# First scan of an SSD kernel: two masks change engines, the scores and the gains are reordered, one weight piece is finished in two steps

## The chip, the cores and the metric

One core of one Trainium2 chip. The metric is the device time of one execution in microseconds (us). Beside the three timed runs there is one profiled execution; its trace gives the start and duration of every instruction.

## The reference, cut to what matters

A Mamba-2 SSD scan over 4 batches of 8 heads, 768 steps, head width 32, state width 16, in chunks of 32; its output, as 3072 rows of 256, goes through a two-layer network with a quick GELU.

```python
cum = np.cumsum(log(clip(a, 1e-6, 1)), axis=-1)         # within a chunk
L = np.exp(cum[..., :, None] - cum[..., None, :]) * causal
y = (C @ B^T * L) @ x + (C @ state) * np.exp(cum)       # inside the chunk, and from the state
state = decay_full * state + sum_j(B_j x_j * decay_from_j)
h = y_rows @ w_in                                       # 256 -> 2048
out = (h * (1 / (1 + np.exp(-1.702 * h)))) @ w_out      # 2048 -> 256
```

The weights arrive as 64-bit floats and are rounded to 32 bits on the chip.

## The kernel before

**Tiles and stages.** The rows are cut into 6 groups of 512 rows; a group is four chunks of 128 rows, and two chunks are a pair. Group 0 is pairs 0 and 1 of batch 0. Its scan has a path of its own, since nothing can hide it: the first 18 us of the span. Then comes `hidden(0, f)` for the 16 blocks f of w_in (two products and one Silu each), then `project_all(0)`, into which the scan of group 1 is put, then groups 1 to 5 with a form that needs fewer products, each with the scan of the next group put in between.

**Order.** Every engine runs its instructions in the order in which the program writes them (`in_order` at the end fixes it). An instruction that waits holds everything behind it on its engine. SP, and at two places ScalarE and GpSimd, issue the DMAs, also in order.

**First scan.** `differ_of` and `decay_exp` (L557) make the decays L of a pair. `turn_first` (L597) transposes B and C on VectorE. `mask_first(p)` (L632) spreads C over the two heads of a row group, on GpSimd. `turn_back` (L609) transposes B back on TensorE, `ends_first` (L478) weighs it with the decay to the end of a half chunk. `score` (L664) makes C B^T of both pairs in one four-bank area `cb`; `since_first` (L515, L520), called between pair 0 and pair 1, makes `since`, the decay from the start. `weigh` (L675) multiplies L by the scores, one VectorE instruction a pair. `gain` (L695) makes A, the increments of the state, of both pairs; `parts_first` (L712) copies them to `steps`, `keep_first` (L717, L725, L726) scans them to the states S. `since_start` (L649) makes CsT on GpSimd. `finish` makes y: `intra` (L818) from L and x, `inter` (L804) from CsT and S; between the two pairs' `intra` stands `fan_all` (L418), which spreads the next pair's decays from the operand X that `pick_a` (L364) made of `az1`. ScalarE copies y to yT (L838). `dense` (L1150) and `pads` (L442) are products of ones whose results nobody reads.

**PSUM banks.** `bank(...)` hands out four banks in turn. In the order of the program the last ones before y are b, rows0, rows1, A0, A1, dense; the four banks of y follow.

**Weights.** They come in pieces: of w_in 0 to 3 with two blocks and 4, 5 with four, of w_out 6 to 9 with four. A piece takes these steps: `fetch` (SP, L181), `fields` (VectorE, L193 and L196: exponent, mantissa), `clamp` (ScalarE, L204 and L205), `rounded` (VectorE, L209), `join` (VectorE, L223 and L229, writes w_in or w_out). `narrow(i)` writes `rounded(i)`, `join(i)` and `fields(i + 1)`: for pieces 2, 4, 5, 6 the join first, for 3 and 7 to 9 `fields(i + 1)` first. Piece 3 is blocks 6 and 7, piece 4 blocks 8 to 11. `fetch(1, held=nc.gpsimd)` begins with a small GpSimd memset of the target (L172), which stands behind `since_start(0)` on GpSimd; SP waits for it, and nine more loads are behind that one on SP's queue.

A table of places, in `in_hidden[0]`, says after which block of `hidden(0, f)` a step is written:

```python
for i, k, c in ((2, 1, 1), (3, 2, 2), (4, 4, 7), (5, 8, 10), (6, 10, 14), (7, 14, 15)):
    at(in_hidden[0], k, lambda i=i: narrow(i))
    at(in_hidden[0], c, lambda i=i: clamp(i + 1))
```

`fold_ident(1)` (L336) fills the second half of a constant of VectorE that the scan of pair 3 reads first, in the projection.

Of the kernel before, what the change touches and what calls it, by code (L numbers as in the profile page):

```python
# [35 lines left out]
def kernel(  # L36
# [99 lines left out]
                out=t[32 * r:32 * r + 32],  # L136
                in_=src[0, Q * r:Q * r + Q, :TG].rearrange("q (i f) n -> i q (f n)", i=32))

    def load(p, parts=None):
        if parts is None:  # L140
            parts = "bcx" if p < 2 * PG else "bx"
            if p >= 2 * PG:
                load_blocks(p)
        for part in parts:
            dst, src, e = {"b": (rb, B, N), "c": (rc, C, N), "x": (rx, x, D)}[part]
            dst[p] = raw.tile([P, 2, NH, e], FP32, tag=part, name=f"{part}{p}",
                              bufs=2 if part == "c" else 3)
            for k in range(2):
                b, c = divmod(2 * p + k, NC)
                sl = slice(c * P, (c + 1) * P)  # L150
                nc.sync.dma_start(out=dst[p][:, k], in_=src[b, :, sl, :].rearrange("h s d -> s h d"))


    assert NF == 4 * CG
# [58 lines left out]

    NEXT = {1: (6,), 5: (9,)}

    def join(i, parts=1):

        name, f, n = PIECES[i]
        n //= parts
        low, m, p2 = bits.pop(i)[1], mantissa.pop(i), power.pop(i)  # L220
        for k in range(parts):
            cols, fs = slice(k * n * DM, (k + 1) * n * DM), slice(f + k * n, f + (k + 1) * n)
            nc.vector.scalar_tensor_tensor(out=p2[:, cols], in0=low[:, cols], scalar=0x80000000,  # L223
                                           in1=p2[:, cols], op0=ALU.bitwise_and, op1=ALU.bitwise_or)
# [4 lines left out]
            nc.vector.scalar_tensor_tensor(  # L229
                out=dst, in0=m[:, cols].bitcast(FP32).rearrange("p (h e) -> p h e", h=h),  # L230
                scalar=2.0 ** -20, in1=p2[:, cols].bitcast(FP32).rearrange("p (h e) -> p h e", h=h),
                op0=ALU.mult, op1=ALU.mult)
        for n in NEXT.get(i, ()):
            fetch(n)

    def narrow(i):
        rounded(i)
        if i in (2, 4, 5, 6):
            join(i, 2 if i in (4, 5) else 1)
        if i == 6:  # L240
            decay_rows(0)
        if i + 1 < len(PIECES):
            fields(i + 1)
        if i not in (2, 4, 5, 6):
            join(i, 2 if i == 3 else 1)


    scratch = dram.tile([NC, 2, NB * NH, H], FP32, name="scratch")
# [41 lines left out]
    load_first("B", [nc.sync] * R)  # L290
    fetch(0)
    load(0, "x")
    load(1, "x")


    edge = const.tile([P, 2], FP32, name="edge")
# [37 lines left out]
    def fold_ident(k, engine=nc.vector):  # L334
# [17 lines left out]
    def clip(t):  # L352

        nc.vector.tensor_scalar(out=t, in0=t, scalar1=1e-6, scalar2=1.0,
                                op0=ALU.max, op1=ALU.min)
        nc.vector.memset(t.rearrange(by_chunk, s=2)[:, :, :, 0], 0.0)
# [65 lines left out]

    def fan_all(p):

        ab = area(f"ab{p}")[:, :, :2 * Q * H]
        for r in range(R):
            fan(p, r, ab[:, r])
        fans[p] = ab

    def decay_fanned(p):  # L430

# [77 lines left out]
    def since_first():  # L509

        since[0] = ssd.tile([P, NC, P], FP32, tag="since", name="since0")
        rows = [bank(f"rows{p}")[:, :2 * P] for p in range(PG)]
        for p in range(PG):
            at = slice(32 * p, 32 * p + 32)
            nc.tensor.matmul(out=rows[p],  # L515
                             lhsT=whose[at, p].rearrange("p h n -> p (h n)"),
                             rhs=cum[at].rearrange("p k s -> p (k s)"), start=True, stop=True,
                             tile_position=(32 * p, 0), skip_group_check=True)
        for p in range(PG):
            nc.scalar.activation(since[0][:, 2 * p:2 * p + 2].rearrange("p c s -> p (c s)"),  # L520
                                 rows[p], AF.Exp)

    def drops():

# [101 lines left out]
    def mask_first(p):  # L626

        s = st[p]
        s["CT"] = ssd.tile([P, 2, Q, P], FP32, tag="CT", name=f"CT{p}")
        if p:  # L630
            nc.vector.memset(s["CT"][:, 0, 0, :1], 0.0)
        nc.gpsimd.tensor_tensor(  # L632
            out=s["CT"], in0=s["tp"].unsqueeze(2).to_broadcast([P, 2, Q, P]),
            in1=part.unsqueeze(1).unsqueeze(3).to_broadcast([P, 2, Q, P]), op=ALU.mult)
# [16 lines left out]
    def score(pairs, between=lambda: None, to=None):  # L651

        cb = (to or area(f"cb{pairs[0]}")).rearrange("p r (k e) -> p r k e", k=2 * PG)
        for n, p in enumerate(pairs):
            s = st[p]
            BT, CT = s["BT"], s.pop("CT")
            s["cb"] = cb[:, :, 2 * n:2 * n + 2]
            if n:
                between()
            for k in range(2):  # L660
                for i, side in enumerate(SIDES):
                    for r in range(R):
                        rows = slice(32 * r, 32 * r + 32)
                        nc.tensor.matmul(  # L664
                            out=s["cb"][side, r, k].rearrange("p (q i) -> p q i", q=Q),
                            lhsT=BT[rows, k, side], rhs=CT[rows, k, :, side],
                            start=True, stop=True, tile_position=(32 * r, H * i),
                            skip_group_check=True)
# [11 lines left out]

        return (4 * p + m + 1) % (2 * NC) == 0

    def gain(pairs, to=None):
# [3 lines left out]
        for n, p in enumerate(pairs):  # L687
            Be = BE.pop(p)[0]
# [12 lines left out]
            increment[p] = [t[:, 2 * n:2 * n + 2] for t in A] if pairs[0] else A  # L701
# [68 lines left out]
    def finish(pairs, steps=range(2)):  # L770
# [38 lines left out]

        def intra(n, p):  # L810
            L = Ls[p]
            for k in range(2):
# [15 lines left out]
        if early:  # L828
            for n, p in enumerate(pairs):
                if n:  # L830
                    fan_all(PG)
                intra(n, p)
            for n, p in enumerate(pairs):
                for i in range(2):
                    inter(n, p, (i,))
            for t in range(NK):
                for i in range(2):
                    nc.scalar.activation(  # L838
                        yT[g][:, t, cols].rearrange("p (k s i) -> p s k i", s=2, i=H)[:, i], y[i][t],
                        AF.Copy)  # L840
# [362 lines left out]
    fields(2)  # L1203
    clamp(2)
    load(PG, "bc")
# [234 lines left out]
```

## Time and profile before

| what | value |
|---|---|
| median of 3 runs | 346.78 us (346.44, 346.78, 349.93) |
| profiled execution | 347.67 us, of it the span 345.9 us |
| granted TensorE clock | 1.00 |
| TensorE busy | 339.2 us, 98% |
| VectorE busy | 256.1 us, 74% (97% from 47 to 80 us) |
| ScalarE busy | 155.1 us, 45% |
| GpSimd busy | 16.7 us, 5% |
| first scan | 0 to 17.89 us |
| hidden layer of group 0 | 17.89 to 46.96 us |

Engines in the trace: PE is TensorE, PEld its weight loads, DVE is VectorE, ACT ScalarE, POOL GpSimd, SP the queue that issues most DMAs; ACTq or SPq is the queue of an engine, where DMAs are issued. A line of the timeline has the start in us, the duration, the engine, the line of the program, the operation with what it writes and reads, and in brackets the time that the engine had waited just before and what ended the wait. An fp32 product is two records of TensorE. A line of the list of waits has who waited for whom, the sum in us, how often, and the longest. A line of the chain of waits has the start, the duration and the step.

### The profile page before, as it was taken

To read this page: it belongs to the slowest core of one execution; us is meant where nothing else is said; L and a number is where in the kernel's file an instruction comes from. 1 tells how busy PE (TensorE), PEld (TensorE's weight loads), DVE (VectorE), ACT (ScalarE), POOL (GpSimd) and SP (SyncE) were. 2 spreads that over 40 slices of the span, in tenths; PEclk is the share of its full clock that TensorE was granted. 3 is DMA by queue.
4 is the path that set the end of the run, shared out by engine and by line. 5 is a ranking of instruction groups with operands and counts; after the bars stand their busy time and mean duration, and the time that the engine had idled before them with its cause. 6 is when DMAs were issued, how large, how long until landed. Compare 5 with 4: busy or idle time off the path is not lost.

```text
span 345.9 us, 8116 instructions
## 1 busy us (share of the span) xinstructions
PE 339.2 (98%) x3380; PEld 270.2 (78%) x3380; DVE 256.1 (74%) x484; ACT 155.1 (45%) x352; POOL 16.7 (5%) x40
## 2 busy tenths in 40 slices
PE   8999999999999999999999999999999999999996
PEld 6633744555788888888888888888888888899996
DVE  5988999999799998858995667787564654465463
ACT  5786771507454324754332554442454322554320
POOL 7300110300000100000000000000000000000000
PEclk9999999999999999999999999999999999999999
DMA  6698899545637100435603036400000300000401
GB/s 160 132 289 211 217 239 133 152 67 102 122 63 127 36 0 15 65 99 100 110 27 51 2 78 121 64 0 3 0 4 2 62 2 0 0 2 0 63 0 62
DMA packets 90004, 25.76 MB, mean 74 GB/s; under 512 B 73416, under 2 KB 87248, under 8 KB 89968
## 3 DMA queue, kind: packets, MB, share of 16 engines
q1 hardware_dynamic: 89104, 24.72, 35.0%
q10 hardware_dynamic: 832, 0.52, 0.5%
q8 instruction: 26, 0.43, 0.5%
q14 instruction: 10, 0.08, 0.1%
q0 software_dynamic: 32, 0.01, 0.0%
HBM read 22.00 MB, written 3.24 MB: 73 GB/s over the span
## 4 chain that ended last, share of the span: by engine, by line
PE 92%; DMA 3%; SPq 2%; DVE 1%; issue 0%; ACT 0%; POOL 0%; DVEq 0%
PE acc L1039 28%; PE X L934 19%; PE Y L944 14%; PE o L976 8%; PE acc L1046 7%; PE h L878 7%; DMA bits<-in_moe_w_in_dram 3%; PE y L818 2%; PE cb L664 2%; SPq L181 1%; PE y L804 1%; PE A L695 1%; PE ab L536 1%; DMA az<-in_a_dram 1%; POOL CsT L649 0%
## 5 line engine op out<-in xcount | busy, mean ns | idle before, releaser
L939 ACT ACTIVATE ac<-X 128x256 f32<-128x256 f32 x76 | 29.1, 383 | 81.7 <-PE X L934 81.0
L1039 PE MATMUL acc<-mg,mw 128*128 128x256 f32 x192 | 54.5, 379 | 0.0
L1066 DVE TENSOR_TENSOR gT<-Y,ac 128x512 f32<-128x512 f32 x38 | 26.2, 689 | 38.1 <-PE Y L944 32.5
L911 ACT ACTIVATE gT<-gT 128x512 f32<-128x512 f32 (+1 forms) x76 | 38.9, 519 | 29.3 <-DVE gT L1066 28.8
L934 PE MATMUL X<-my,mi 128*128 128x256 f32 x152 | 45.2, 380 | 0.0
L1039 PEld LDWEIGHTS acc<-mg,mw 128*128 128x128 f32 x192 | 36.6, 190 | 4.9
L1066 DVE TENSOR_TENSOR gT<-Y,b 128x256 f32<-128x256 f32 x38 | 15.8, 419 | 28.5 <-PE Y L944 28.5
L878 PE MATMUL h<-yT,w_in 128*128 128x512 f32 (+1 forms) x92 | 35.5, 541 | 1.4 <-DVE w_in L229 0.9
L1039 PE MATMUL acc<-gT,w_out 128*128 128x256 f32 x128 | 35.5, 380 | 0.0
L878 PEld LDWEIGHTS h<-yT,w_in 128*128 128x128 f32 x92 | 17.2, 190 | 18.2 <-issue 12.8
L934 PEld LDWEIGHTS X<-my,mi 128*128 128x128 f32 x152 | 28.0, 190 | 4.0 <-ACT ac L939 0.3
L976 PE MATMUL o<-gT,w_out 128*128 128x512 f32 x64 | 28.3, 596 | 0.0
L902 DVE TENSOR_TENSOR mg<-gT 128x512 f32<-128x512 f32 x40 | 27.2, 681 | 0.0
L1039 PEld LDWEIGHTS acc<-gT,w_out 128*128 128x128 f32 x128 | 24.3, 190 | 3.4 <-ACT yT L853 0.2
L939 ACT ACTIVATE b<-X 128x256 f32<-128x256 f32 x38 | 14.6, 383 | 20.8 <-PE X L934 20.3
L934 PE MATMUL X<-yT,w_in 128*128 128x256 f32 x76 | 23.2, 389 | 0.0
L944 PE MATMUL Y<-yT,w_in 128*128 128x256 f32 x76 | 22.7, 381 | 0.0
L944 PE MATMUL Y<-my,mi 128*128 128x256 f32 x76 | 22.7, 381 | 0.0
L934 PE MATMUL X<-my,w_in 128*128 128x256 f32 x76 | 22.5, 380 | 0.0
L944 PE MATMUL Y<-yT,mi 128*128 128x256 f32 x76 | 22.5, 380 | 0.0
L976 PEld LDWEIGHTS o<-gT,w_out 128*128 128x128 f32 x64 | 11.9, 190 | 13.6 <-issue 12.7
L408 DVE TENSOR_TENSOR_SCAN L<-a,idents 128x1024 f32<-128x1024 f32 x9 | 20.5, 2279 | 0.3 <-DMA a<-scratch 0.3
(152 smaller groups left out, 547.8 us busy)
## 6 DMA issues: line engine op xcount, KB each, us to landing
a<-scratch SPq DMA_DIRECT2D x18, 256.0 KB, 4.9
bits<-in_moe_w_out_dram SPq DMA_DIRECT2D x8, 512.0 KB, 7.4
x<-in_x_dram SPq DMA_DIRECT2D x24, 128.0 KB, 3.7
out_dram<-ob SPq DMA_DIRECT2D x40, 64.0 KB, 2.0
bits<-in_moe_w_in_dram SPq DMA_DIRECT2D x8, 256.0 KB, 3.7
bits<-in_moe_w_in_dram SPq DMA_DIRECT2D x4, 512.0 KB, 11.4
b<-in_B_dram SPq DMA_DIRECT2D x20, 64.0 KB, 3.3
af<-in_a_dram SPq DMA_DIRECT2D x3, 384.0 KB
```

The lines of the kernel that those rows point to most:

```text
L408: nc.vector.tensor_tensor_scan(out=L, data0=ra[p].rearrange("p k e -> p (k e)"), data1=idents.rearrange("p h i -> p (h i)"), initial=0.0, ...
L664: nc.tensor.matmul(out=s["cb"][side, r, k].rearrange("p (q i) -> p q i", q=Q), lhsT=BT[rows, k, side], rhs=CT[rows, k, :, side], start=Tru ...
L878: nc.tensor.matmul(out=h[:, cols], lhsT=w_in[:, f, k], rhs=yT[g][:, k, cols], start=(k == 0 and c == 0), stop=(k == NK - 1), skip_group_ch ...
L902: nc.vector.tensor_tensor(out=t[:, 0:2], in0=B[:, :, 1], in1=B[:, 0], op=ALU.subtract)
L911: nc.scalar.activation(o, i, AF.Silu, scale=GELU_SCALE)
L934: nc.tensor.matmul(out=s["X"], lhsT=lhsT, rhs=rhs, start=i == "1", stop=i == "4", skip_group_check=True)
L939: nc.scalar.activation(copy, s["X"], AF.Copy)
L944: nc.tensor.matmul(out=o, lhsT=lhsT, rhs=rhs, start=s.pop("new", False), stop=i != "5", skip_group_check=True)
L976: nc.tensor.matmul(out=o[c], lhsT=w_out[:, c, f], rhs=gT[g, f // 2][:, f % 2], start=(f == 0), stop=(f == NF - 1), skip_group_check=True)
L1039: nc.tensor.matmul(out=acc[g][0][i][:, cols], lhsT=w, rhs=h[:, cols], start=(j == 0 and k == 0 and (i, 0) in begins), stop=(j == NF // 2 - ...
L1046: nc.tensor.matmul(out=o[k] if type(o) is list else o[:, cols], lhsT=h[:, cols], rhs=w, start=(j == 0 and (i, k) in begins), stop=(j == NF ...
L1066: nc.vector.tensor_tensor(out=o, in0=v, in1=w, op=ALU.add)
```

## The change

- `load(1, "x")`: its first half stays on SP's queue, its second half is issued by ScalarE's queue, behind the load of the Exp table.
- `mask_first(1)` on GpSimd becomes `mask_blocks(1)` on ScalarE (two activations); the VectorE memset in front of it is gone. `clip(az1)` goes from VectorE to GpSimd, and `pick_a` from ScalarE (two activations) to GpSimd (one product of 128x512).
- `since_first` stands ahead of both scores. Then come the score of pair 0, the gain of pair 0, the score of pair 1, the gain of pair 1; the two weighings follow the gains.
- `dense(8, bank("dense"))` becomes `dense(4, free)`, in the unused half of a bank of `since_first`, so the four banks of y are then two that held the rows and two that held A. A second `dense(4, free)` stands behind the last `inter`, in the unused half of the fan's area.
- `intra` of the first scan runs over heads outside and chunks inside.
- `join(1)` is in two halves; piece 3's join is in two halves around `fields(4)`; `clamp(4)` stands behind block 3 instead of block 2. `fold_ident(1)` moves from the first scan to the front of piece 6's join. The next fetches stay behind the last half of a join.

```diff
-    def load(p, parts=None):
+    def load(p, parts=None, ks=range(2), queue=nc.sync):
...
     def narrow(i):
         rounded(i)
         if i in (2, 4, 5, 6):
+            if i == 6:
+                fold_ident(1)
             join(i, 2 if i in (4, 5) else 1)
         if i == 6:
             decay_rows(0)
+        if i == 3:
+            join(i, 2, (0,))
         if i + 1 < len(PIECES):
             fields(i + 1)
-        if i not in (2, 4, 5, 6):
-            join(i, 2 if i == 3 else 1)
+        if i == 3:
+            join(i, 2, (1,))
+        elif i not in (2, 4, 5, 6):
+            join(i)
...
     load(0, "x")
-    load(1, "x")
+    load(1, "x", (0,))
...
     table(AF.Exp)
+    load(1, "x", (1,), nc.scalar)
...
-        for q in range(Q):
-            nc.scalar.activation(X[:, :, q], az1, AF.Copy, scale=pick1[:, q:q + 1])
+        nc.gpsimd.tensor_tensor(
+            out=X, in0=az1.unsqueeze(2).to_broadcast([P, 2, Q, P]),
+            in1=pick1.unsqueeze(1).unsqueeze(3).to_broadcast([P, 2, Q, P]), op=ALU.mult)
...
-        rows = [bank(f"rows{p}")[:, :2 * P] for p in range(PG)]
+        whole = [bank(f"rows{p}") for p in range(PG)]
+        rows = [t[:, :2 * P] for t in whole]
...
+        return whole[0][:, 2 * P:]
...
-            for k in range(2):
-                for h in range(NH):
+            for h, k in [(h, k) for h in range(NH) for k in range(2)] if early else [
+                    (h, k) for k in range(2) for h in range(NH)]:
...
                 if n:
-                    fan_all(PG)
+                    free = fan_all(PG)[:, 0, 2 * Q * H:]
                 intra(n, p)
             for n, p in enumerate(pairs):
                 for i in range(2):
                     inter(n, p, (i,))
+            dense(4, free)
...
-    clip(az1)
...
-    mask_first(1)
+    mask_blocks(1)
+    clip(az1, nc.gpsimd)
     pick_a(PG)
...
-    score(range(PG), since_first, to)
+    free = since_first()
+    scores = score_steps(range(PG), to)
+    next(scores)
+    gain(range(PG), between=lambda: [None for _ in scores])
     weigh(0)
     weigh(1)
     drops()
-    gain(range(PG))
...
-    dense(8, bank("dense"))
+    dense(4, free)
     finish(range(PG))
     join(0, 2)
-    fold_ident(1)
...
-    join(1)
+    join(1, 2)
...
-    for i, k, c in ((2, 1, 1), (3, 2, 2), (4, 4, 7), (5, 8, 10), (6, 10, 14), (7, 14, 15)):
+    for i, k, c in ((2, 1, 1), (3, 2, 3), (4, 4, 7), (5, 8, 10), (6, 10, 14), (7, 14, 15)):
```

More of the change, by code (lines that the diff above doesn't have):

```diff
@@ L145, in load @@
             dst, src, e = {"b": (rb, B, N), "c": (rc, C, N), "x": (rx, x, D)}[part]
-            dst[p] = raw.tile([P, 2, NH, e], FP32, tag=part, name=f"{part}{p}",
-                              bufs=2 if part == "c" else 3)
-            for k in range(2):
+            if 0 in ks:
+                dst[p] = raw.tile([P, 2, NH, e], FP32, tag=part, name=f"{part}{p}",
+                                  bufs=2 if part == "c" else 3)
+            for k in ks:
                 b, c = divmod(2 * p + k, NC)
                 sl = slice(c * P, (c + 1) * P)
-                nc.sync.dma_start(out=dst[p][:, k], in_=src[b, :, sl, :].rearrange("h s d -> s h d"))
+                queue.dma_start(out=dst[p][:, k], in_=src[b, :, sl, :].rearrange("h s d -> s h d"))
     assert NF == 4 * CG
@@ L214, with join @@
     NEXT = {1: (6,), 5: (9,)}
-    def join(i, parts=1):
+    def join(i, parts=1, only=None):
         name, f, n = PIECES[i]
         n //= parts
-        low, m, p2 = bits.pop(i)[1], mantissa.pop(i), power.pop(i)
-        for k in range(parts):
+        low, m, p2 = bits[i][1], mantissa[i], power[i]
+        for k in range(parts) if only is None else only:
             cols, fs = slice(k * n * DM, (k + 1) * n * DM), slice(f + k * n, f + (k + 1) * n)
@@ L232, in join @@
                 op0=ALU.mult, op1=ALU.mult)
-        for n in NEXT.get(i, ()):
-            fetch(n)
+        if only is None or parts - 1 in only:
+            for t in bits, mantissa, power:
+                t.pop(i)
+            for n in NEXT.get(i, ()):
+                fetch(n)
     def narrow(i):
@@ L350, with clip @@
     fans, flat = {}, {}
[L352 to L356, printed above, removed]
+    def clip(t, engine=nc.vector):
+        engine.tensor_scalar(out=t, in0=t, scalar1=1e-6, scalar2=1.0,
+                             op0=ALU.max, op1=ALU.min)
+        engine.memset(t.rearrange(by_chunk, s=2)[:, :, :, 0], 0.0)
     def pick_a(p):
@@ L423, in fan_all @@
     def fan_all(p):
-        ab = area(f"ab{p}")[:, :, :2 * Q * H]
+        whole = area(f"ab{p}")
+        ab = whole[:, :, :2 * Q * H]
         for r in range(R):
@@ L428, in fan_all @@
         fans[p] = ab
+        return whole
     def decay_fanned(p):
@@ L629, in mask_first @@
         s["CT"] = ssd.tile([P, 2, Q, P], FP32, tag="CT", name=f"CT{p}")
-        if p:
-            nc.vector.memset(s["CT"][:, 0, 0, :1], 0.0)
         nc.gpsimd.tensor_tensor(
@@ L649, in since_start, with score, score_steps @@
         engine.tensor_tensor(out=s["CsT"], in0=tp, in1=since[b][:, c:c + 2], op=ALU.mult)
-    def score(pairs, between=lambda: None, to=None):
+    def score(pairs, to=None):
+        for step in score_steps(pairs, to):
+            pass
+    def score_steps(pairs, to=None):
         cb = (to or area(f"cb{pairs[0]}")).rearrange("p r (k e) -> p r k e", k=2 * PG)
@@ L658, in score @@
             if n:
-                between()
+                yield
             for k in range(2):
@@ L681, in last_chunk, with gain @@
         return (4 * p + m + 1) % (2 * NC) == 0
-    def gain(pairs, to=None):
+    def gain(pairs, to=None, between=lambda: None):
         A = [(bank(f"A{pairs[0]}_{i}") if to is None else to[:, i, TG // 2:])[
@@ L687, in gain @@
         for n, p in enumerate(pairs):
+            if n:
+                between()
             Be = BE.pop(p)[0]
@@ L811, in intra @@
             L = Ls[p]
-            for k in range(2):
-                for h in range(NH):
+            for h, k in [(h, k) for h in range(NH) for k in range(2)] if early else [
+                    (h, k) for k in range(2) for h in range(NH)]:
                     for i, side in enumerate(SIDES):
```

## The prediction

> **What bounds the kernel now.** I read the page first: TensorE is busy 98% of the span, and its row in the 40 slices shows under 9 tenths only at the two ends.
>
> ```profile
> PE   8999999999999999999999999999999999999996
> ```
>
> So an edit in the first scan or the first hidden layer pays only through what TensorE waits there. Next the list of who waits for whom, TensorE's own rows:
>
> ```profile
> PE h L878 <- DVE w_in L229: 0.9, 1, 0.9
> PE h L878 <- ACT yT L838: 0.5, 1, 0.5
> PE cb L664 <- POOL CT L632: 0.4, 1, 0.4
> ```
>
> The longest after the start is one wait of 0.9 us for a weight block. TensorE's timeline places it; the same list from 30 us on holds only this row, so from 29.52 TensorE never waits, and what it gains before then should reach the end.
>
> ```profile
> 17.89 10.78 PE L878 MATMUL h<-yT,w_in 128*128 128x512 f32 x24 [0.51 <-ACT yT L838]
> 29.52 17.43 PE L878 MATMUL h<-yT,w_in 128*128 128x512 f32 x52 [0.85 <-DVE w_in L229]
> ```
>
> The 24 records are blocks 0 to 5 (four per block, 0.43 apart, 1.72 a block): block 6 begins at 29.52. The chain of waits up to 60 us says why:
>
> ```profile
> 17.15 9.61 DMA bits<-in_moe_w_in_dram
> ...
> 27.28 0.69 DVE p L193
> 27.98 0.61 DVE m L196
> 28.58 0.34 DVE p L223
> ...
> 28.95 0.44 DVE w_in L229
> ```
>
> L193 and L196 split piece 4 (blocks 8 to 11); L223 and L229 finish piece 3 (blocks 6, 7). Block 6 needs nothing of piece 4, but stands behind it on VectorE. The timeline of all engines shows both sides:
>
> ```profile
> 25.91 0.72 ACT L205 ACTIVATE p<-p,edge 128x512 uint32<-128x512 f32 x1
> ...
> 27.28 0.69 DVE L193 TENSOR_SCALAR p<-bits 128x1024 uint32<-128x1024 uint32 x1 [1.10 <-DMA bits<-in_moe_w_in_dram]
> ...
> 30.09 1.22 DVE L209 SCALAR_TENSOR_TENSOR m<-bits,m 128x1024 f32<-128x1024 uint32 x1
> ...
> 31.22 0.69 DVE L223 SCALAR_TENSOR_TENSOR p<-bits,p 128x512 uint32<-128x512 uint32 x1
> ```
>
> Piece 3 has its exponents at 26.63; its join could have run in VectorE's idle 1.10.
>
> **First scan, TensorE and VectorE.** From the timeline:
>
> ```profile
> 9.99 1.04 POOL L632 TENSOR_TENSOR CT<-Ct,part 128x512 f32<-128x512 f32 x1 [1.14 <-DVE CT L631]
> 10.69 0.66 ACT L520 ACTIVATE since<-rows 128x256 f32<-128x256 f32 x2 [0.38 <-PE rows L515]
> 11.08 0.70 PE L664 MATMUL cb<-CT,Bt 32*64 32x128 f32 x32 [0.43 <-POOL CT L632]
> 11.88 2.35 DVE L675 TENSOR_TENSOR L<-L,cb 128x1024 f32<-128x1024 f32 x2 [0.31 <-PE cb L664]
> 13.55 0.93 PE L818 MATMUL y<-L,x 64*32 64x64 f32 x64
> 15.56 0.84 PE L818 MATMUL y<-L,x 64*32 64x64 f32 x63 [0.30 <-issue]
> ```
>
> TensorE's new order from 9.33: rows 0.68 (chain, 10.03 to 10.71), score of pair 0 0.62 (9.40 to 10.03), A of pair 0 0.40 (half of 11.71 to 12.50), score of pair 1 0.62: last score issued at 11.65, where it was 11.08 + 0.62 = 11.70. The half of C for pair 1 comes from ScalarE, two activations like those of the pick (both over from 9.38 to 10.31), ready near 10.31, before its use at 11.03. Pair 0's weighing waits for the last score in the trace (score 0 was over at 10.03, the wait ends at 11.88), so both weighings move only 0.05, to 11.83. VectorE loses the clip (0.54 + 0.06) and a memset (0.06), but this only lengthens its wait for the score: nothing. Scan, S and the first join keep their times less 0.05: first join at 15.86 (15.91).
>
> The first y products lose their wait: two of their four banks are now those of the rows instead of A's, and the loop by heads uses these two first. They start at 13.05 (11.83 + 1.22) instead of 13.55. But the fan and the second y products need the second weighing, over at 14.2 as before, and S at 15.9; the 0.30 marked issue has no shown cause and stays. Hidden begins between 17.45 and 17.89; I take 17.75. The half dense removed saves 0.43, which was under the wait; the one added behind y (two records of 0.22) lies in the 0.51 that TensorE waits for yT, and costs at most 0.43 without that cover.
>
> **GpSimd and the queues.** GpSimd ends pair 0's C at 8.86 and then has the clip (not in the trace on this engine: 0.31 as a memset of this shape, up to 1.02 as the slower two-input CsT; I take 0.6, between the two affine selects of this shape, 0.44 and 0.84), a small memset 0.1 and the pick, 1.04 like C. CsT then starts at 10.6 to 11.05; since is ready near 10.73 (rows sooner, ScalarE's order unchanged in length), against 11.15. Behind CsT stands the memset that releases SP's weight loads, so these start 0 to 0.3 sooner than 12.23. I count nothing of it. SP loses one of four x issues (3.43 / 4 = 0.86), done long before. On ScalarE's queue the issue costs 0.49 (three C loads took 1.48) to 0.86; it falls under the table load, as the C loads did (2.23 to 3.71 beside a load from 2.16). Without that cover, exp of pair 0 moves from 7.08 to at most 7.26, and the next exps wait for TensorE at 8.31 anyway.
>
> **Hidden layer, VectorE and ScalarE in turn.** Join 0 ends at 17.52. fold_ident (0.69) is gone here, so fields 1 runs 17.45 to 18.2 (its load issued at 12.65 landed near 17.1, by the 4.0 median of two). ScalarE's exponents of piece 1 start behind yT at 18.0, end 19.5 (18.55 to 20.03 before). Join 1, now in halves of 0.42 + 0.42: block 2 ready at 20.4 (21.48), block 3 at 21.2; the split costs 0.26. Fields 2 at 21.1 (21.40), exponents to 23.05, block 4 ready at 24.5 (24.78), fields 3 at 24.4, exponents to 26.35, join of block 6 26.4 to 27.2 (29.38). Only then fields 4, 27.15 to 28.45, by then landed (26.76 plus the 0.5 to its first use). Block 7 is ready at 29.2, rounding of piece 4 29.15 to 30.4, exponents 28.0 to 30.35 (two of 1.15), join of blocks 8, 9 30.45 to 31.8.
>
> TensorE: block 0 at 17.75, 2 at 21.2, 4 at 24.65, 6 at 28.1, 8 wanted at 31.5 and ready at 31.8: it begins at 31.9. Before, it was 29.52 + 3.44 = 32.96. **Gain 1.1 us.** The waits from 17.89 to 29.52 are 1.31 (11.63 less six blocks of 1.72), and with the start 0.14 sooner 1.45 are to be had; 0.4 of it goes at block 8, which takes the place of block 6. Clamp 4, moved behind block 3's silu, no longer holds ScalarE's silus while it waits for piece 4 (0.90 at 28.01).
>
> **Later.** VectorE leads by 0.6 from block 8; fold_ident in front of join 6 lies in its wait of 0.53 there and takes 0.16 of that. Blocks 12 to 15 of w_out have the least slack: ready at 69.45, used at 70.30. 0.85 plus 0.45 covers the 1.1. The rest of the span shifts whole.
>
> **The sum.** Span 345.9 - 1.1 = 344.8; the profiled execution took 347.67, 1.77 above its span and 0.89 above the median 346.78 (346.44 to 349.93). I forecast from the median: 346.78 - 1.1 = 345.7.
>
> **Rivals.** (a) x comes too late. A of pair 0 now stands ahead of score 1, so pair 0's x, first read at 11.71 before, is wanted at 10.63, and one x load of pair 1 enters ahead of it. For: the DMA engines are full (share 1.05 to 1.27 from 7 to 10 us). Against: issued from 5.51 and landing after 3.6, it is there near 10. If all four land together at 11.7, the weighings and all that hangs on them slip by 1.05 and the gain is 0.05: 346.7; half of it, 346.2. The Trainium skill (DMA: Bandwidth & Descriptors, Issuing engines are not separate DMA queues) says that DMAs of several engines share the same 16 and interleave, so that only issue time is saved; it speaks for this rival, and the trace agrees so far as one queue alone fills the engines.
>
> (b) Slower: piece 4 lands later. Its load is the seventh in a row behind GpSimd's memset, and one issue in this row already took 1.90 (12.65 to 14.54) with nothing shown to hold it, while the engines moved 53 GB/s. Each us of landing after 27.0 moves block 8 by one; from a landing at 27.9 the kernel is slower. A second such stall gives 28.7, block 8 at 33.75, +0.8: 347.6. For: GpSimd has 1.7 more work ahead of the release. Against: it had waited 1.14 in that place, and its end comes out no later.
>
> (c) TensorE's clock. One dense matmul less, in other places. At half clock the first blocks would take 3.44 each, and block 8 would come at 35, +2: 348.8. Against: granted 1.00 in every us from 4 to 30, with waits up to 0.85. The Trainium skill (TensorE: Matmul & The Clock Gate, What's actually happening) puts the halving after an idle window of some 3.4 us; no wait here comes near it.
>
> (d) Nothing moves: the wait leaves block 6 and returns whole at block 8 or w_out: 346.8.
>
> (e) More: weight loads sooner and the stall of 1.90 gone. Then VectorE still caps block 8 unless S comes sooner too; with no wait at all from 17.45, block 8 at 31.2, gain 1.75: 345.0.
>
> **How the numbers follow.** Forecast 0.60 (its own range 345.2 to 346.2), (a) 0.14, (b) 0.09, (c) 0.03, (d) 0.07, (e) 0.07. The range runs from (e) to (b): 344.9 to 347.6, some 0.07 out below and 0.08 above. 1%, about what a measurement of this kernel can tell from no change, is 3.5 us; a case beyond it needs (c) worse than worked out, or a gain that no wait in the trace offers: faster 0.03, within 0.93, slower 0.04.
>
> **What would show it.** Right: block 6 without a wait near 28, a short wait at block 8 near 31.9, fields 4 behind the join of block 6, the weighing still at 11.8 to 11.9, y products at 13.05. Wrong: A or the second score waiting for x; block 8 waiting for fields 4 on the DMA; a wait at the projection near 70; a first weight load later than 12.3.

## The result, and the profile after

| | before | after |
|---|---|---|
| median of 22 runs each, same chip | 346.83 us | 348.70 us |
| lowest to highest | 346.34 to 349.93 us | 347.73 to 354.27 us |
| profiled execution, of it the span | 347.67 us, 345.9 us | 348.73 us, 347.0 us |
| first hidden layer begins, ends | 17.89, 46.96 us | 19.16, 48.04 us |

The ratio is 1.0046, with an interval of 1.0030 to 1.0062: slower by about 1.6 us, where 1.1 us less was forecast. Times are compared between undisturbed executions; the two profiles of the kernel that has only the second queue are of executions of 500 and 1231 us, and are not used. In both profiles of the table 299 us lie between the end of the hidden layer and the end of the span (345.9 - 46.96, 347.0 - 48.04), so the whole difference arises in the scan and the first hidden layer: the layer begins 1.27 us later, and ends 1.08 later. This is the list of TensorE's waits after, without those of the first 9 us:

```profile
PE h L899 <- PE h L899: 0.9, 1, 0.9
...
PE y L838 <- DVE L L693: 0.4, 1, 0.4
PE A L715 <- DMA x<-in_x_dram: 0.4, 1, 0.4
PE cb L682 <- issue: 0.3, 1, 0.3
PE y L838 <- issue: 0.2, 1, 0.2
```

No wait for a weight block is left: what the change was to remove is gone. In its place stand a wait for x, one for the weighing (L693) and three stops for which no semaphore answers: "issue", and an h that waits for an h, which is the same thing between two records of one group. The timeline of the same kernel places them:

```profile
8.93 1.26 POOL L365 TENSOR_SCALAR az<-az 128x256 f32<-128x256 f32 x1
...
11.47 0.35 PE L715 MATMUL A<-x,Be 64*32 64x64 f32 x16 [0.38 <-DMA x<-in_x_dram]
11.75 0.65 PE L682 MATMUL cb<-CT,Bt 32*64 32x128 f32 x19
12.55 0.09 POOL L173 MEMSET bits<- 128x1 uint32 x1
...
12.67 0.47 PE L682 MATMUL cb<-CT,Bt 32*64 32x128 f32 x13 [0.27 <-issue]
...
13.22 2.35 DVE L693 TENSOR_TENSOR L<-L,cb 128x1024 f32<-128x1024 f32 x2 [1.19 <-PE cb L682]
...
16.66 1.01 PE L838 MATMUL y<-L,x 64*32 64x64 f32 x64 [0.25 <-issue]
...
19.16 1.98 PE L899 MATMUL h<-yT,w_in 128*128 128x512 f32 x4
...
22.00 14.43 PE L899 MATMUL h<-yT,w_in 128*128 128x512 f32 x33 [0.85 <-PE h L899]
```

A of pair 0 waits 0.38 for x, and the second score behind it stops after 19 of its 32 records, so the weighings begin at 13.22 instead of 11.88; the hidden layer stops after block 0 and from 22.00 runs without a stop (the 33 records reach to the end of the window asked for, past blocks 6 and 8). The chain of waits goes through the same places:

```profile
6.00 5.42 DMA x<-in_x_dram
...
11.47 0.35 PE A L715 x16
11.82 0.58 PE cb L682 x19
12.39 0.27 issue
...
21.16 0.84 issue
```

### What the stops are

TensorE's records (a product and its weight load are one each), counted from the start of the program, stop at the same counts in every kernel that stops: at about 448, 704 and 960, 256 apart (some records are missing from each trace, here up to 12 by the third count, so the count is good to that). The page's list of queues has a queue for them:

```profile
q8 instruction: 26, 0.43, 0.5%
```

26 packets in 0.43 MB, which the trace gives as 16,384 bytes each: one such packet for each 256 records. The packets' own times, read from the same traces, against the records at the three counts:

```
                     packet for 448   at 448          packet for 704   at 704          packet for 960   at 960
                     start  end       last   next     start  end       last   next     start  end       last   next
before               8.69   10.13     11.83  11.84    12.82  14.16     15.06  15.56    18.16  19.08     21.00  21.53
after                9.75   11.27     12.13  12.67    14.30  15.63     16.04  16.66    19.50  20.39     20.55  22.00
```

(us; "last" and "next" are the starts of the records on both sides of the count.) A packet starts 1.0 to 2.8 us after TensorE entered the block ahead of it ("next" of one column to "start" of the following: 11.84 to 12.82, 16.66 to 19.50). It takes 0.9 to 1.5, and where TensorE stopped, it went on 1.0 to 1.6 us after the packet's end (14.16 to 15.56, 11.27 to 12.67, 15.63 to 16.66, 20.39 to 22.00). By these times TensorE stops where it gets there sooner, and since the next packet starts only behind the border, the delay is handed on. The last step of the kernel before (21.00 to 21.53, 0.1 more than the usual 0.43) came 2.4 us after the packet's end and is not explained by this. So the 0.30 us marked "issue" before the second y products of the kernel before, and the 0.85 after block 0 now, fit one mechanism: instructions that had not arrived. The Trainium skill (Runtime: NRT & Kernel Launch, Instruction fetch mechanics) says that the sequencer fetches the next block of 256 instructions while the present one runs and that crossing a border is mostly hidden; blocks of this size agree with the trace, but in this scan, where 256 records take 3 to 4 us, the crossing is not hidden: it cost up to 1.7 us in the runs below.

### The profile page after: what moved, and what is told of

Same layout as the page of the kernel before. It is cut to its first block, busy times and chain, and to the rows that moved or that the text cites. A ratio compares the mean times of both kernels' runs of the same rounds, so it can differ in the third digit from the quotient of the medians.

```text
span 347.0 us, 8124 instructions
## 1 busy us (share of the span) xinstructions
PE 339.7 (98%) x3382; PEld 270.6 (78%) x3382; DVE 256.2 (74%) x483; ACT 155.1 (45%) x352; POOL 18.9 (5%) x42
## 4 chain that ended last, share of the span: by engine, by line
PE 95%; DMA 2%; SPq 1%; issue 1%; DVE 0%
PE acc L1060 28%; PE X L955 19%; PE Y L965 14%; PE h L899 10%; PE o L997 8%; PE acc L1067 7%; PE y L838 3%; PE cb L682 2%; PE y L824 2%; DMA x<-in_x_dram 2%; PE A L715 1%; SPq L135 1%; SPq L288 0%; DVE L L693 0%; SPq L182 0%
```

## The experiments

Theories after the result: the stops come from the second DMA queue for x; from the new order (A of pair 0 ahead of the second score, with its wait for x); from the count at which the borders fall; or they were there before and the hidden part alone gains what was forecast. All ratios are to the kernel before on the same chip, in brackets the 95% interval.

### First four: order, queue, hidden part, borders

**Both scores ahead of the gains**, as before, the rest as after:

```diff
-    next(scores)
-    gain(range(PG), between=lambda: [None for _ in scores])
+    for _ in scores:
+        pass
+    gain(range(PG))
```

> The changed kernel with both scores ahead of both gains again (all else of the change kept). Theory X+F: in the changed kernel A of pair 0 waits for x until 11.43 in front of the second score, and TensorE's record 448 (its instructions come in blocks of 256 records: gaps without a shown cause stand behind records 448, 704 and 960) falls into the second score. Both then come behind the scores: the weighings start at 11.8 to 11.9 instead of 13.22, block 8 near 32, span 344.7 to 345.2 (changed kernel 347.0, before 345.9). Rival H, the hidden-layer part is at fault: weighings earlier, but span stays above 346.5. Rival Q, the x load on ScalarE's queue is at fault by itself: A still waits, now behind the scores, and the span stays above 346.

Measured 1.0057 (1.0026 to 1.0087). Three of the 12 runs had a mean clock of 0.995 or less; the other nine alone are at 1.0029 of before, and the change without its runs of that kind is at 1.0042. The weighings came back to 12.00, but the stops stayed and moved: 0.58 in A, 1.01 in the second y products, a step of 0.62 at 960 where 0.43 is usual, and the hidden layer began at 19.02. So the order is at most a small part of the loss (0.13%); most of the gain hoped for from the earlier weighings was taken by the next stop.

**All of x on SP's queue**, the rest as after:

```diff
-    load(1, "x", (0,))
+    load(1, "x")
...
-    load(1, "x", (1,), nc.scalar)
```

> The changed kernel with all of x on SP's queue again, the gain of pair 0 still ahead of the second score. Theory X+F with the queue as cause: x of pair 0 lands before 11.0, the block behind record 448 is fetched near 8.7 as before (9.75 in the changed kernel), the second score has no gap: weighings at 12.0 to 12.3, span 345.3 to 346.0. If the order alone is the cause (x of pair 0 is late on any queue): weighings stay at 13.0 or later, span 346.8 or more.

Measured 1.0015 (1.0004 to 1.0026), against 1.0046 with the queue: the queue is 0.31% of the change, 1.1 us. TensorE's timeline of this kernel has no stop marked "issue" in the scan, and the hidden layer begins where it did before, with a short wait at block 8:

```profile
11.99 0.74 PE L714 MATMUL A<-x,Be 64*32 64x64 f32 x32
...
17.87 14.12 PE L898 MATMUL h<-yT,w_in 128*128 128x512 f32 x32
32.26 14.00 PE L898 MATMUL h<-yT,w_in 128*128 128x512 f32 x44 [0.28 <-DVE w_in L230]
```

**The hidden part alone**: the kernel before with the joins in halves, the clamp and the fold moved, and nothing of the scan.

```diff
+        if i == 3:
+            join(i, 2, (0,))
         if i + 1 < len(PIECES):
             fields(i + 1)
...
-    join(1)
+    join(1, 2)
...
-    for i, k, c in ((2, 1, 1), (3, 2, 2), ...
+    for i, k, c in ((2, 1, 1), (3, 2, 3), ...
```

> The kernel before with the hidden-layer part alone: join 1 and piece 3 in halves, the first half of piece 3 ahead of fields 4, clamp 4 behind block 3, fold_ident in front of join 6; the first scan is that of before. My sum (the first scan is at fault): block 6 without a wait near 28.4, block 8 begins near 32.0, span 344.8 to 345.2. Rival H (this part brings nothing or loses): span 345.7 or more, with a wait of 1 us or more at block 8 or later.

Measured 0.9991 (0.9982 to 1.0000), 346.65 us: the best of all kernels tried, but 0.3 us, not 1.1. TensorE's timeline has the layer in one piece, no wait at 6 or 8:

```profile
17.75 28.24 PE L887 MATMUL h<-yT,w_in 128*128 128x512 f32 x76 [0.50 <-ACT yT L847]
```

**Without the 9 products of ones** (`pads`, 36 records) that stand ahead of the scan's transposes, so that each border falls 36 records later in the work; the rest as after:

```diff
     to = area("cb0")
-    pads(9, to[:, 0])
     turn_back()
```

> The changed kernel without the nine small products of ones ahead of the transposes (18 products and 18 weight loads in the trace, results not used). Theory F: the boundary behind record 448 moves by 36 records out of the second score into the gain of pair 1, and the one behind 960 out of block 1 into a later block: the second score loses its gap (12.40 to 12.67), weighings at 12.6 to 12.8 instead of 13.22, no wait at block 1, span 346.3 to 346.6. Theory X alone (the gaps belong to the data, not to the count of records): both gaps stay where they are, weighings at 13.2, span 347.0.

Measured 1.0137 (1.0092 to 1.0182), the slowest. The borders at 448 and 704 were passed without a stop (12.92 and 16.38). This does not show that their place did it: the packet for 448 was also over sooner (10.57 instead of 11.27), and TensorE came later, since x was waited for 0.94 us. A new stop of 1.1 us came at 149.8 us, far from the scan. Part of the ratio is a lost piece of clock, told at the end: the two of its six runs at full clock are at 1.0067.

### Second four: the queue alone, the noise of one execution

**Only the queue**, on the kernel before:

```diff
-    load(1, "x")
+    load(1, "x", (0,))
...
     table(AF.Exp)
+    load(1, "x", (1,), nc.scalar)
```

> The kernel before with one thing of the change alone: the second half of pair 1's x issued on ScalarE's queue. Theory F (the x packets of two queues delay the loads of TensorE's instruction blocks, which come every 256 records): the first block load in the scan starts near 9.7 instead of 8.7, gaps without a shown cause appear behind records 448 (in A), 704 and 960; hidden begins 0.5 to 1.2 later; span 345.9 to 347 (before: 345.4 as the median of the runs beside this), time 1.002 to 1.005 of before. If the queue alone is harmless: span 345.4, gaps as before, ratio 1.000 +- 0.001.

Measured 1.0075 (1.0049 to 1.0100): a loss of 2.6 us by the queue alone, more than in the change. Three of the ten runs behind this ratio had a mean clock of 0.995 or less; the other seven alone are at 1.0062. There is no profile to compare; the same kernel once more,

> The kernel before with x's second half of pair 1 on ScalarE's queue, once more: the first profile of it is of an execution whose clock was reduced all through. If the queue costs through the order of landings and block loads: in this profile a wait for x or gaps behind records 448, 704 or 960, hidden beginning at 18.4 or later (17.9 in the kernel before), ratio 1.003 to 1.008. If the first ratio (1.0075) came of the disturbed chip: ratio 1.000 to 1.002, hidden from 17.9.

gave 1.0087 (1.0059 to 1.0114), from two executions, and again no profile to compare.

**x on SP and both scores ahead**, the rest as after:

```diff
-    load(1, "x", (0,))
+    load(1, "x")
...
-    load(1, "x", (1,), nc.scalar)
...
-    next(scores)
-    gain(range(PG), between=lambda: [None for _ in scores])
+    for _ in scores:
+        pass
+    gain(range(PG))
```

> The changed kernel with x on SP's queue and both scores ahead of the gains. If the order still costs once x is on SP (second score 0.3 late behind A of pair 0): weighings 11.8 to 11.9 instead of 12.17, span 344.6 to 345.0, ratio 0.999 or less, near the hidden-layer part alone. If the order is harmless then: as with x on SP alone, span 345.7 as the median of the runs, ratio 1.001 to 1.002; the rest of the loss is then in the other parts of the first scan (engines, dense products) and in the 0.2 us that these kernels take outside the span.

Measured 1.0047 (1.0025 to 1.0069), no better than x on SP alone. Its profiled execution, one of its longest (350.02 us, where the median is 348.11), had x late (1.8 us of waits in A) and a packet for 448 that ended at 11.16, although only one queue carried x: a late packet needs no second queue.

**The kernel before, unchanged, for a second profile**:

> The kernel before once more, for a second profile of it. If my size for the hidden part (1.1) was read from an execution with a longer wait than usual, this one has a shorter wait at block 6 than 0.85 or a hidden layer that ends before 46.79, and a span near 345.4. If not, both are as in the first profile (span 345.9).

Measured 346.59 us, span 344.9, and the wait at block 6 is not there. The timeline:

```profile
17.90 28.16 PE L878 MATMUL h<-yT,w_in 128*128 128x512 f32 x76 [0.51 <-ACT yT L838]
...
26.29 0.69 DVE L193 TENSOR_SCALAR p<-bits 128x1024 uint32<-128x1024 uint32 x1
```

Fields of piece 4 run at 26.29, not 27.28: SP issued its ten weight loads in 6.67 us here, in 8.18 in the first profile, where one issue had taken 1.90. So the 0.85 us that most of the forecast was made of does not stand in every execution. A long issue early in this row is no accident of one profile, though: it took 1.90 in the first, 1.25 in the second, 1.24 in the hidden part alone and 1.68 in the change; what differs is its length.

**x on SP, without the products of ones** (to the kernel with x on SP):

```diff
-    pads(9, to[:, 0])
```

> The changed kernel with x on SP's queue and without the nine small products of ones. With the pads but x on ScalarE's queue 5 of 22 runs had a mean clock of 0.995, without the pads 4 of 6; with x on SP and the pads none of 12. If the clock falls because of the pads' place alone: some runs have a mean clock of 0.995 or less, 3 to 5 us longer. If it takes the waits for x and for instructions as well: every run near 1.000, span 345 to 346.

Measured 1.0076 (1.0053 to 1.0099), from four runs, one of them with a mean clock of 0.995, and with the same late stop, 0.9 us at 149.9.

### The other parts, one at a time

**The engine moves on the hidden part**: C of pair 1 to ScalarE, clip and pick to GpSimd.

```diff
-    clip(az1)
...
-    mask_first(1)
+    mask_blocks(1)
+    clip(az1, nc.gpsimd)
     pick_a(PG)
```

> The kernel before with the hidden-layer part and, of the first scan, only the three moves between engines: pair 1's half of C on ScalarE, the clip and the pick on GpSimd. GpSimd's clip took 1.26 in the changed kernel (0.54 on VectorE), and its first memset for the weight loads came at 12.55 instead of 12.11. If these moves cost: ratio above the 0.999 of the hidden-layer part alone, 1.000 to 1.002, memset at 12.4 or later, and the 0.2 us more outside the span is here. If they are harmless: ratio 0.998 to 0.999, time less span 1.73.

Measured 1.0014 (1.0000 to 1.0028), 0.23% above the hidden part. GpSimd's timeline:

```profile
9.05 1.31 POOL L363 TENSOR_SCALAR az<-az 128x256 f32<-128x256 f32 x1
...
11.90 0.89 POOL L657 TENSOR_TENSOR CsT<-Ct,since 128x256 f32<-128x256 f32 x1 [0.26 <-ACT since L530]
12.73 0.10 POOL L172 MEMSET bits<- 128x1 uint32 x1
```

The memset that releases SP's weight loads is 0.62 later than before (12.11), and two weight blocks were waited for (0.49 and 0.27 us). The chain of waits runs through it and the load into the blocks, but it comes from `since` on ScalarE and not from the clip or the pick:

```profile
11.46 0.37 ACT since L530
...
11.90 0.89 POOL CsT L657
...
13.27 5.35 DMA bits<-in_moe_w_in_dram
...
18.71 0.44 DVE p L193
...
21.15 0.43 DVE w_in L229
```

GpSimd had waited 0.26 for `since`, and this whole execution began later: the transposes stood at 9.51, in the kernel before at 8.75. Counted from them the memset came at 3.22, before at 3.36, in the hidden part alone at 3.08. So this trace does not show that the moves delayed the loads by more than 0.14 us.

**The order, the halves of `dense` and y by heads on the hidden part**, no engine moved, x on SP:

```diff
-    score(range(PG), since_first, to)
+    free = since_first()
+    scores = score_steps(range(PG), to)
+    next(scores)
+    gain(range(PG), between=lambda: [None for _ in scores])
...
-    gain(range(PG))
...
-    dense(8, bank("dense"))
+    dense(4, free)
```

> The changed kernel with x on SP's queue and the three moves between engines undone: what stays of the first scan is the order (rows, score 0, A 0, score 1, A 1), the two half dense products, the y products by heads. If this part costs: ratio 1.001 to 1.003, and the 0.2 us more outside the span is here (time less span 1.95 instead of 1.73). If it is harmless: 0.998 to 0.999, 1.73.

Measured 1.0005 (0.9990 to 1.0021): 0.14% above the hidden part, with intervals that overlap; no gain.

**The queue on the hidden part**, the same edit as for the queue alone, on the kernel of 0.9991:

> The kernel before with the hidden-layer part, and the second half of pair 1's x on ScalarE's queue. If the queue costs by itself, as x back on SP suggested (1.0046 to 1.0015): ratio 1.002 to 1.008 where the hidden-layer part alone has 0.9991, and the profile shows where: hidden from 18.4 or later, behind a wait for x, for TensorE's next block of instructions (records 448, 704, 960), or a later first score. If it does not: 0.998 to 1.000 and hidden from 17.8 to 18.1.

Measured 1.0050 (1.0023 to 1.0077): 0.59%, 2.1 us, for 128 KB on another queue. Its nine runs lie between 347.20 and 350.46 us, and the profile is of one of the longest (350.29). The list of waits, then TensorE's timeline:

```profile
PE h L889 <- issue: 1.7, 1, 1.7
PE y L829 <- issue: 1.3, 1, 1.3
PE A L706 <- issue: 0.7, 1, 0.7
```

```profile
12.90 0.69 PE L706 MATMUL A<-x,Be 64*32 64x64 f32 x44 [0.72 <-issue]
...
17.57 0.84 PE L829 MATMUL y<-L,x 64*32 64x64 f32 x63 [1.28 <-issue]
...
24.87 24.65 PE L889 MATMUL h<-yT,w_in 128*128 128x512 f32 x69 [1.70 <-issue]
```

No wait for x stands in the list; what was late are the instructions. The packet for 448 ended at 11.53; the next two started 2.3 and 4.9 us after TensorE entered the blocks ahead of them (15.18 after 12.90, 22.47 after 17.57), the last amid the weight loads, and ended at 16.14 and 23.46: each stop ends 1.4 us after a packet's end. Without the queue the three packets were over at 10.37, 13.87 and 19.18, and the list of waits has no such row.

**The clip back on VectorE**, the other engine moves kept:

```diff
     turn_first("B")
+    clip(az1)
...
-    clip(az1, nc.gpsimd)
     pick_a(PG)
```

> The kernel with the hidden-layer part and the three moves between engines (1.0014, time less span 2.04), with the clip back on VectorE at its old place. If GpSimd's clip (1.26 to 1.31 in the traces) is the cost: GpSimd's memset at 12.2 or sooner, time less span 1.73, ratio 0.998 to 1.000. If the pick or the mask is: time less span 2.0, ratio 1.001 or more.

Measured 1.0004 (0.9986 to 1.0022) against 1.0014 (1.0000 to 1.0028) with it: some 0.1%, which the intervals don't separate. The time less span was 1.90, between the two values expected. GpSimd's memset stood at 11.96, but this execution began sooner too (transposes at 8.89): counted from them it came at 3.07, with the clip on GpSimd at 3.22. No weight block was waited for.

**The hidden part without the products of ones** (`pads(9, to[:, 0])` taken out):

> The kernel before with the hidden-layer part, without the nine small products of ones. The changed kernel lost 0.9% without them, 0.6% with x on SP. If they matter through the clock (TensorE idle from 8.2 to 8.7): ratio 1.004 or more, with mean clocks of 0.995 or less in some runs or a later grant of the clock in the profile. If they matter only where the boundary of the instruction blocks falls badly: 0.998 to 1.001, clock 1.000.

Measured 1.0055 (1.0026 to 1.0084). The hidden layer is whole (17.96 to 46.1), but behind it the list of waits, which is empty there with them, has:

```profile
PE y L827 <- issue: 1.2, 1, 1.2
PE A L704 <- DMA x<-in_x_dram: 0.4, 1, 0.4
```

36 records fewer at the start move every later border. One of them now falls into a dense run of small products, near record 3482 at 149.85 us, and TensorE goes on at 151.24:

```profile
151.24 0.73 PE L827 MATMUL y<-L,x 64*32 64x64 f32 x49 [1.17 <-issue]
```

The packet for this border ended at 149.83, again 1.4 us ahead; in the other two kernels without the products of ones it is the same (149.66 and 151.03, 149.55 and 151.00). One of the nine runs had a mean clock of 0.995; the other eight alone are still at 1.0045, so the price is there without a loss of clock, which neither branch of the expectation had. Of the 2.2 us by which this kernel is slower than the hidden part alone, the trace gives 1.2 to this stop and 0.4 to a wait for x; the rest is smaller pieces.

**A candidate**: the hidden part with C of pair 1 on ScalarE, the rows first, the pick on GpSimd behind the release of the loads, the clip on VectorE.

```diff
-    mask_first(1)
-    pick_a(PG)
+    mask_blocks(1)
...
-    score(range(PG), since_first, to)
+    since_first()
+    score(range(PG), to=to)
...
     since_start(1, nc.gpsimd)
+    pick_a(PG)
```

> The hidden-layer part with pair 1's half of C on ScalarE, the rows ahead of both scores, the pick on GpSimd behind the release of the weight loads, the clip on VectorE, x on SP. If the moves hold up: weight loads from 11.6 to 11.9, weighings at 11.5 to 11.8, ratio 0.996 to 0.999. If TensorE's instruction blocks bound the scan (record 704, the second y products, not before 15.4): hidden still from 17.6 to 17.9, ratio 0.998 to 1.000.

Measured 1.0045 (1.0017 to 1.0073), though its profiled span was 345.2 and its weighings began at 11.42, the earliest of all. A waited 0.61 us for x instead, the hidden layer still began at 17.86, as the second branch of the expectation has it, and the spans of the other runs at full clock went up to 348.6 (two more had lost clock). It is no better than the hidden part alone.

## Why the prediction was wrong

**The hidden layer: mechanism right, size wrong.** Fields 4 went behind the first half of piece 3's join, the wait at block 6 went away, block 8 became the next bound (0.28 us in the kernel with x on SP), and the rest shifted whole. But the term "gain 1.1 us" was mis-sized: alone it measured 0.9991, 0.3 us (at most 0.6). It was taken from a profile whose span, 345.9, was 1.0 above the second profile of the same kernel, and that profile had no such wait. The prediction saw the sign of it, an issue of 1.90 us "with nothing shown to hold it", and used it only as a danger for the new kernel, not as a doubt of the wait that this stall had caused. (The 53 GB/s that it puts beside this issue are those of 14 to 15 us; over 12.65 to 14.54 the engines moved 139.)

**The second queue: priced at its issue only.** "On ScalarE's queue the issue costs 0.49 to 0.86; it falls under the table load" is true (0.46 us, and the next exponential began at 7.09 instead of 7.08), but this is the term that the sum put at nothing, and the largest one that failed. Cost: 0.31% in the change, 0.59% on the hidden part, 0.75% on the kernel before. Rival (a) had quoted the rule that speaks against it (the Trainium skill, DMA: Bandwidth & Descriptors, Issuing engines are not separate DMA queues: all share the same 16 engines and interleave), and the trace agrees: x moves in 4096 packets of 128 bytes; from 8 to 10 us 1024 of them were those of ScalarE's queue, beside 1817 of SP's, and pair 0's second half landed at 11.43. But the main loss was not the wait for x: on the hidden part the queue cost 0.59% with no such wait, and in the change moving the second score ahead of that wait again brought back little.

**"The 0.30 marked issue has no shown cause and stays."** This is the step in which the mechanism failed. The stop itself stayed (0.25 at the same place), but by the packets' times it had a cause, late instructions, and this did not stay at one place: in the kernel before, the packet for 448 was over at 10.13, with the 1.4 us that lie between a packet's end and the record after a stop that is 11.53, and TensorE came there at 11.84: 0.3 us of slack. After, the packet ended 1.14 later, and TensorE stopped at this border too. With that, the wait for x and the new order the weighings slipped from 11.88 to 13.22 (11.83 forecast; 12.17 with x on SP, without the stop), the first y products began at 14.59 (13.05 forecast), and the next two borders were hit later in turn, the last at the price of 0.85.

**GpSimd.** The clip was put at 0.6 with bounds of 0.31 and 1.02; it took 1.26, outside both. So the loads were released at 12.67, 0.44 later, not 0 to 0.3 sooner. In the change itself no weight block was waited for, so this cost nothing there; alone, the engine moves cost 0.23%, 0.8 us. Of it 0.2 to 0.3 us is no part of the span: the time around it (time less span, mean of the runs) was 1.73 us before and 1.74 in the hidden part alone, 1.92 to 2.04 in all kernels with the clip on GpSimd, 1.88 to 1.90 with only the pick there. The prediction took this difference as fixed.

The moves also touched VectorE, which the prediction put at "nothing". VectorE's rounding of piece 0 stands right ahead of the weighings. In the hidden part alone it took 0.68 us, in the change 1.50, while GpSimd's pick ran beside it (10.44 to 11.48). With x on SP the weighings began right at its end, with no wait for the score; first that kernel, then the hidden part alone:

```profile
10.63 1.50 DVE L210 SCALAR_TENSOR_TENSOR m<-bits,m 128x512 f32<-128x512 uint32 x1
12.17 2.35 DVE L692 TENSOR_TENSOR L<-L,cb 128x1024 f32<-128x1024 f32 x2
```

```profile
10.84 0.68 DVE L209 SCALAR_TENSOR_TENSOR m<-bits,m 128x512 f32<-128x512 uint32 x1
```

In the candidate, which has the pick later, the rounding took 0.68 again. That the pick slows it is inferred from these times.

**The parts**: hidden -0.09%, engine moves and order together +0.24% (1.0015 against 0.9991), queue +0.31%, sum +0.46%. They are steps from one kernel to the next, so they add up by construction. Against the forecast, the miss of 2.7 us (345.7 forecast, 1.0046 of 346.83 is 348.4) is the gain that measured 0.3 instead of 1.1 (0.8), the moves and the order put at nothing (0.8), and the queue put at nothing (1.1). The engine moves (+0.23) and the order (+0.14) were not additive one by one, within intervals of about 0.15% each way.

**Rivals.** (a) came in part, by 0.38 us of wait for x, but undoing the order did not cure it. (b), (d) and (e) did not come: piece 4 was in time, and the wait did not return. (c) is not in the profile, though 5 of the 22 runs had a mean clock of 0.995. None of them had the mechanism that decided, and the range reached only as far as their prices.

**Left open**: why the queue costs twice as much on the kernel before as within the change (also in runs at full clock alone, 0.62% against 0.26%); why the time outside the span is longer with more work on GpSimd, and what makes up the rest of the moves' price; what of the order's 0.14% is real. That packets of x on two queues are what holds the instruction packets back is inferred from their times (the packet for 448 ended from 9.9 to 10.6 us in nine profiles without the queue and from 11.2 to 11.5 in three with it, but also at 11.07 and 11.16 in two without and at 10.57 in one with it); no run held an instruction packet back by itself.

## What to carry to other kernels

Before a wait of under 1 us in one profile is made the target, take a second profile of the same kernel: if the span differs by that much, the wait may belong to the execution. An "issue" stop on an engine that issues several hundred small instructions within some microseconds is to be counted in records: if the stops are 256 apart, as here, look for the packets of the instruction queue and compare their ends with the stops. What moves the borders or the packets, here 128 KB on another queue or products that nobody reads, then has a price that no list of dependencies shows. Price a DMA that is moved to another queue by what its packets meet, not by its issue.

## What the hardware showed that was not expected

- A stop at a border of 256 records cost 0.3 to 1.7 us here, and one late border passes its delay to the next two (0.72, 1.28, 1.70 with the queue on the hidden part).
- A clip of 128x256 in fp32 took 0.53 to 0.58 us on VectorE and 1.25 to 1.33 on GpSimd, some 2.3 times as long. The Trainium skill (GPSIMD Engine Reference, Engine selection) gives a factor of about 2 for two inputs and calls one input roughly line rate; this one has one input.
- Removing 36 records ahead of 9 us brought a stop of 0.9 to 1.2 us at 150 us, in all three kernels without them, each 1.4 us behind the end of an instruction packet.
- VectorE's rounding of 128x512 took 0.68 us in the candidate and 1.50 in the change, where GpSimd's product of 128x512 ran beside it.
- In 5 of 22 runs of the change, and 4 of 6 of it without the products of ones, the mean granted clock was 0.99 to 0.995 and the span 349 to 352 us, also in 3 of 12 runs with both scores ahead; among the runs of the kernel before beside the experiments it was 1 in 106. No profile caught the moment, so its place is not known.
